# Softmax on Trainium2: the normalization fused with the split of the probabilities into two float16 parts

## The chip, the cores and the metric

The kernel runs on one core of a Trainium2 chip. The metric is the device time of one execution in microseconds (us); the time of a kernel is the median of its runs. The engines are named as the profile names them: PE (TensorE, matrix products; PEld is its weight load), DVE (VectorE), ACT (ScalarE), POOL (GpSimd) and SP (SyncE, which issues every DMA of this kernel). SBUF is the core's working memory, PSUM the memory into which PE writes.

## What is computed

Attention with a causal window of 128 keys and a linear bias, then two gated blocks. Cut to what matters:

```python
scores = (q @ k.T) / sqrt(64)                       # 4 batches, 8 heads, 576 tokens, 64 features
scores = where(mask, scores + bias, -1e9)            # mask: the query's own key and the 127 before it
attn = exp(scores - max(scores, axis=-1))
attn = attn / (sum(attn, axis=-1) + 1e-9)
x = attn @ v                                         # then heads side by side: [2304, 512]
x = (x @ w_a) * (x @ w_b) @ w_out                    # 512 -> 1536 -> 512
x = ((x @ w1) * (x @ w2) @ w3) @ w_out2              # 512 -> 1024 -> 1024 -> 512
```

The change concerns the division by the sum and what makes `attn` ready for the product with `v`.

## The kernel before

Attention is cut into 16 units (a batch and a pair of heads), and each unit into 5 steps of up to 128 query rows; there are 80 steps. The two heads of a pair are the index `j`. In steps 1 to 3 of a unit each head has 128 queries against 256 keys, so that its tile is 128x256; in step 0 there are 128 keys (128x128 for each head); in the last step 64 queries of both heads lie below each other in one 128x256 tile. So a unit has 7 head tiles of 128x256 and 2 of 128x128, and the kernel has 112 and 32 of them.

One step runs through these functions and lines:

- `scores` (L313): PE forms the scores in PSUM.
- `exps`: DVE adds the bias and takes the row's extremum (L325, with a short read of the accumulator after it), ACT takes the exponential and its sum (L331). The result is `pe`, float32, in SBUF; the statistics are in `st`.
- `norms`: two short DVE instructions turn the sum into the factor `st` (L344, L347). The factor holds a power of two that `pv_out` takes out again.
- `probs`: DVE multiplies `pe` by the factor in place (L357, one instruction for each head). The product is then split into two float16 parts that stand in `pp`: the first is a rounded copy (L363, on ACT; L361, on DVE, in step 0 alone), the second is what the copy lacks (`sub` on POOL, recorded at the helper's line L73, as are other subtractions: those of `v`, of the weights, of the gated product). A DMA then transposes `pp` into `pt` (L366).
- `pv` (L388): PE multiplies `pt` with three parts of `v`. `pv_out` (L400 on ACT, L401 on DVE) writes the token rows for the gated blocks, again as a rounded part and a rest.

The tiles `pe`, `st`, `pp` and `pt` have 4 buffers each, the scores 3 PSUM banks. Beside this, DVE and ACT split the transposed q and k (`qkh`, `qkl`, L278, L279), POOL splits `v` (128x640, two instructions for each unit), six weight tiles are converted (L107 to L132, tiles `ca` and `ce`), and PE does products of the first gated block where attention leaves it room (`Filler`, L521 to L551).

In which order the steps' functions are written down is set by `attention_ops`: the probabilities of a step come two steps after its scores, the product with `v` eight steps after them. From that, a scheduler of the programming layer sets the order of every engine's queue by a modelled timeline, so an edit to one instruction can move many others. Each engine works through its own queue in order. All transposes and loads stand in SP's queue.

After attention the kernel converts the other weights on ACT, DVE and POOL (L107 to L132), forms `w3 @ w_out` (L439) and runs the gated blocks (L521, L541, L559).

Of the kernel before, what the change touches and what calls it, by code (L numbers as in the profile page):

```python
# [15 lines left out]
ACTF = mybir.ActivationFunctionType  # L16
# [4 lines left out]
# Float32 products run as three float32r passes: an operand x is the exact sum of  # L21
# hi = float32r(x) and lo = x - hi, and x*w = lo*hi' + hi*lo' + hi*hi' to float32's accuracy.
# The second block's w3 @ w_out is formed first: (g @ w3) @ w_out = g @ (w3 @ w_out).
# Weights come as float64: their words are put together as rounded float32 on the chip.
# [6 lines left out]
GROUPS = (6, 4)  # groups of two 128-column chunks of each block's inner features  # L31
TA, TN = 256, 512  # tokens of a tile: beside attention, and after it
HALF = 1280  # the token at which the accumulators are cut in two
LAG, NLAG = 8, 2  # steps of attention from the scores to the product with v, and to the norms
AT = (0, 0, 1, 3)  # steps of a unit at which the next one is transposed
V_AT = {2: 1, 6: 2}  # steps at which the second and the third unit's v are loaded
FILL = 0.75  # microseconds of the first group's products in a step of attention
PACE = (0.3, 0.6)  # turns of the weights' conversion in a step: the first batch, the others
TURN = 400  # tokens of a chunk for each turn later
# [4 lines left out]
def attention_moe_moe(ctx, tc, q, k, v, w_a, w_b, w_o, w_1, w_2, w_3, w_o2, out):  # L44
# [27 lines left out]
    def sub(eng, out, a, b):  # L72
        eng.tensor_tensor(out=out, in0=a, in1=b, op=ALU.subtract)  # L73
# [5 lines left out]
    # ---------------------------------------------------------------- weights  # L79
    def load_cols(w, c):  # L80
        """128 columns of a [512, .] weight: [128, 4 * 128] with the rows on 4 x 128 partitions."""
# [7 lines left out]
    def load_rows(w, r, c):  # L89
        """128 rows and 512 columns."""  # L90
# [7 lines left out]
    def convert(raw, hi=None, lo=None, use=()):  # L98
        """Float64's two words as float32, to the nearest (0 below float32's exponents), and its
        split: stages, to be emitted one after the other, each when the one before has run."""  # L100
# [41 lines left out]
    class Stages:  # L142
        """Parts (load, stages of what it loads): a part's stages are emitted in turns one after
        the other, its load ahead of them; its second stage is the last to read the load."""
# [33 lines left out]
    # ---------------------------------------------------------------- attention  # L178
# [16 lines left out]
    def consts():  # L195
# [5 lines left out]
        # c - p - 128 for key column c of the window and query row p  # L201
# [13 lines left out]
        # the bias of each head, as the unscaled scores take it: a power of 2 times up to 8 bits  # L215
# [4 lines left out]
        # and for the two heads of a pair below each other  # L220
# [14 lines left out]
    def load_unit(u, which=(0, 1, 2)):  # L235
        b, hp = units[u]
        for x in which:
# [13 lines left out]
            # the last block of q has its two heads on the diagonal, zeros beside them  # L251
# [4 lines left out]
    # q's blocks and k's side by side, as many of them at a time as a bank takes  # L256
# [4 lines left out]
    def prep(u):  # L261
        """Functions that transpose and split a unit's q, k and v: (tensor engine, others)."""
# [20 lines left out]
        def v_parts():  # L283
            # v's three bfloat16 parts: the upper half of v, of what is left of it, and of what is left then
# [12 lines left out]
    def window(i):  # L297
        """Query rows, keys and key blocks of a query block; the groups of heads that it has side
        by side: the last block's rows are half as many, its two heads fill the partitions."""
        m = P if i < NB - 1 else LAST  # L300
        nb = 1 if i == 0 else 2
        return m, nb * P, nb, 2 if m == P else 1
# [451 lines left out]
```

## Time and profile before

| | |
|---|---|
| median of 3 runs | 1056.13 us (1048.25 to 1060.08) |
| the profiled execution, first to last instruction | 1056.7 us |
| attention, up to its last product with `v` | about 282 us |
| busy over the whole span | PE 1017.9, DVE 691.0, ACT 382.0, POOL 494.3 us |
| instructions on POOL | 409 |

The profiled execution is 0.6 us longer than the median, so its times can be set against the median as they stand. A busy time is the time in which an engine had at least one instruction under way; a PE that is busy is not PE at its peak, since its instructions overlap and may run at either of two clocks (2.4 GHz where the granted clock is 1.00, 1.2 GHz where it is 0.5; a stretch with both lies between). A wait of an engine costs only if the engine is the one that others wait for, so the chain of waits is read beside the busy times.

### The profile page before, as it was taken

The numbers are of one execution on the slowest core, as the hardware profiler recorded it, in microseconds if no ns is written. First come the engines' busy times: TensorE is split into PE (matmuls) and PEld (weight loads), VectorE is DVE, ScalarE is ACT, GpSimd is POOL, SyncE is SP. The second block draws the span as 40 slices with busy tenths as digits, with TensorE's granted clock in tenths as the row PEclk, the third lists the DMA queues.
The fourth block names the chain that finished last, engine by engine and source line by source line (L and its number), as shares of the span: only waits on it lengthen the run. The fifth ranks groups of instructions, "written<-read, shape, count | busy, mean of one in ns | idle before, by whom it ended". The sixth has DMA issues, their size and how long they took to land.

```text
span 1056.7 us, 16482 instructions
## 1 busy us (share of the span) xinstructions
PE 1017.9 (96%) x6162; PEld 838.2 (79%) x6162; DVE 691.0 (65%) x1420; ACT 382.0 (36%) x929; POOL 494.3 (47%) x409
## 2 busy tenths in 40 slices
PE   7889999999999889999999999999999999999998
PEld 5567788787987778887788788888888888888886
DVE  6999997757499995587969659565273373322222
ACT  5555766655344232332333323233322221211110
POOL 6566645445267562264636226477572352421111
PEclk9688979878899899999999999999999999999999
DMA  6867676656333221232232223121021020000012
GB/s 140 170 122 154 118 114 121 123 101 115 81 100 100 79 100 70 74 107 73 99 109 84 77 71 99 60 80 41 1 80 40 20 81 20 20 1 1 11 70 100
DMA packets 160080, 85.23 MB, mean 81 GB/s; under 512 B 128000, under 2 KB 148992, under 8 KB 160000
## 3 DMA queue, kind: packets, MB, share of 16 engines
q1 hardware_dynamic: 160000, 84.18, 31.5%
q8 instruction: 48, 0.79, 0.3%
q14 instruction: 32, 0.26, 0.1%
HBM read 58.20 MB, written 8.91 MB: 64 GB/s over the span
## 4 chain that ended last, share of the span: by engine, by line
PE 62%; DVE 22%; DMA 6%; issue 6%; ACT 2%; POOL 1%; SPq 1%; DVEq 0%; ACTq 0%; POOLq 0%
PE mm L521 33%; PE mm L559 10%; PE mm L541 7%; DVE ca L117 4%; PE tr L388 4%; PE mm L439 4%; PE s L313 3%; DVE pe L357 3%; DVE ca L120 3%; DVE ca L113 2%; DVE ce L123 2%; DMA pt<-pp 2%; DVE ce L127 2%; DMA raw<-in_moe_w_out 1%; DVE pe L325 1%
## 5 line engine op out<-in xcount | busy, mean ns | idle before, releaser
L73 POOL TENSOR_TENSOR gl<-g,gh 128x512 fp32r<-128x512 f32 (+1 forms) x108 | 127.7, 1183 | 265.3 <-ACT gh L531 258.4
L132 POOL TENSOR_TENSOR ca<-ca,ce 128x512 f32<-128x512 f32 x76 | 104.7, 1378 | 138.2 <-DVE ce L127 127.4
L528 DVE TENSOR_TENSOR g<-a,mm 128x512 f32<-128x512 f32 (+1 forms) x108 | 64.1, 594 | 157.3 <-PE mm L521 146.7
L531 ACT ACTIVATE gh<-g 128x512 fp32r<-128x512 f32 (+1 forms) x108 | 60.4, 559 | 209.4 <-DVE g L528 209.1
L73 POOL TENSOR_TENSOR pp<-pe,pp 128x512 f16<-128x512 f32 (+1 forms) x80 | 81.8, 1030 | 73.1 <-ACT pp L363 39.9
L521 PE MATMUL mm<-x_hi,wlA 128*128 128x512 f32 (+1 forms) x464 | 109.2, 356 | 0.0
L521 PE MATMUL mm<-x_lo,whA 128*128 128x512 f32 (+1 forms) x464 | 106.9, 351 | 0.0
L521 PE MATMUL mm<-x_hi,whA 128*128 128x512 f32 (+1 forms) x464 | 106.2, 349 | 0.0
L521 PE MATMUL mm<-x_hi,wlB 128*128 128x512 f32 (+1 forms) x400 | 99.8, 371 | 5.5 <-DVE g L528 5.0
L526 ACT ACTIVATE a<-mm 128x512 f32<-128x512 f32 (+1 forms) x108 | 56.1, 519 | 126.6 <-PE mm L521 126.5
L521 PE MATMUL mm<-x_lo,whB 128*128 128x512 f32 (+1 forms) x400 | 98.8, 369 | 0.0
L521 PE MATMUL mm<-x_hi,whB 128*128 128x512 f32 (+1 forms) x400 | 98.7, 369 | 0.0
L521 PEld LDWEIGHTS mm<-x_lo,whA 128*128 128x128 f32 x464 | 80.3, 197 | 10.5
L521 PEld LDWEIGHTS mm<-x_hi,whA 128*128 128x128 f32 x464 | 79.7, 196 | 11.1
L113 DVE TENSOR_SCALAR ca<-ca 128x512 f32<-128x512 f32 x76 | 48.8, 642 | 60.4 <-ACT ca L107 60.4
L521 PEld LDWEIGHTS mm<-x_hi,wlA 128*128 128x128 f32 x464 | 78.6, 195 | 12.1 <-issue 0.6
L107 ACT ACTIVATE ca<-raw 128x512 f32<-128x512 f32 x76 | 50.9, 669 | 101.5 <-DMA raw<-in_moe_w 51.6
L521 PEld LDWEIGHTS mm<-x_hi,wlB 128*128 128x128 f32 x400 | 70.6, 188 | 19.9 <-DVE g L528 6.1
L117 DVE SCALAR_TENSOR_TENSOR ca<-raw,ca 128x512 int32<-128x512 int32 x76 | 82.4, 1084 | 1.6
L357 DVE TENSOR_SCALAR pe<-pe,st 128x256 f32<-128x256 f32 (+1 forms) x144 | 81.5, 602 | 1.3
L331 ACT ACTIVATE pe<-pe,st 128x256 f32<-128x256 f32 (+1 forms) x144 | 68.7, 478 | 37.6 <-DVE st L325 36.0
L120 DVE SCALAR_TENSOR_TENSOR ca<-raw,ca 128x512 int32<-128x512 int32 x76 | 80.9, 1065 | 1.5
(100 smaller groups left out, 2086.7 us busy)
## 6 DMA issues: line engine op xcount, KB each, us to landing
raw<-in_moe_w SPq DMA_DIRECT2D x32, 512.0 KB, 3.5
raw<-in_moe_w_out SPq DMA_DIRECT2D x20, 512.0 KB, 3.5
raw<-in_moe_w_a SPq DMA_DIRECT2D x12, 512.0 KB, 3.5
raw<-in_moe_w_b SPq DMA_DIRECT2D x12, 512.0 KB, 3.5
out<-acc SPq DMA_DIRECT2D x18, 256.0 KB, 2.0
q_raw<-in_q SPq DMA_DIRECT2D x32, 128.0 KB, 2.6
k_raw<-in_k SPq DMA_DIRECT2D x32, 128.0 KB, 2.8
v_raw<-in_v SPq DMA_DIRECT2D x32, 128.0 KB, 2.6
```

The lines of the kernel that those rows point to most:

```text
L73: eng.tensor_tensor(out=out, in0=a, in1=b, op=ALU.subtract)
L113: nc.vector.tensor_scalar(out=a, in0=a, scalar1=bits(0x38100000), scalar2=bits(0x3FFFFFF8), op0=ALU.is_ge, op1=ALU.mult,)
L117: nc.vector.scalar_tensor_tensor(out=ai, in0=hw, scalar=3, in1=ai, op0=ALU.logical_shift_left, op1=ALU.bitwise_and)
L120: nc.vector.scalar_tensor_tensor(out=ai, in0=hw, scalar=-(1 << 30), in1=ai, op0=ALU.bitwise_and, op1=ALU.bitwise_or)
L132: nc.gpsimd.tensor_tensor(out=a, in0=a, in1=es[0], op=ALU.add)
L331: nc.scalar.activation(pe[:, j, :n], pe[:, j, :n], ACTF.Exp, bias=st[:, 0, j:j + 1], scale=-1.0, accum_out=st[:, 1, j:j + 1],)
L357: nc.vector.tensor_scalar(out=pe[:, j, :n], in0=pe[:, j, :n], scalar1=st[:, j:j + 1], scalar2=None, op0=ALU.mult)
L521: nc.tensor.matmul(p, w[:, z, kk, :], x[:, kk, o], start=(y == 0), stop=(y == len(terms) - 1))
L528: nc.vector.tensor_tensor(out=gg, in0=a, in1=ps[1], op=ALU.mult)
L531: nc.scalar.activation(gh, gg, ACTF.Copy)
L541: nc.tensor.matmul(p, w, x, start=(y == 0), stop=(y == len(terms) - 1))
L559: nc.tensor.matmul(p, x, w, start=(y == 0), stop=(y == len(terms) - 1))
```

## The change

The multiplication in place goes. The first float16 part becomes a copy with the factor as the copy's scale, one instruction for each head: on ACT in steps 1 to 4, on DVE in step 0 (`tensor_scalar` with a float16 output). The second part becomes one DVE instruction for each head, which multiplies `pe` by the factor and subtracts the first part (`scalar_tensor_tensor`). POOL has no part in the probabilities any more. The diff also drops comments, which is left out here.

```diff
 def probs(u, i):
     ...
         for j in range(nj):
-            nc.vector.tensor_scalar(
-                out=pe[:, j, :n], in0=pe[:, j, :n], scalar1=st[:, j:j + 1], scalar2=None, op0=ALU.mult
-            )
-        if i == 0:
-            nc.vector.tensor_copy(out=pp[:, :, 0, :], in_=pe[:, 0:nj, :n])
-        else:
-            nc.scalar.activation(pp[:, :, 0, :], pe[:, 0:nj, :n], ACTF.Copy)
-        sub(nc.gpsimd, pp[:, :, 1, :], pe[:, 0:nj, :n], pp[:, :, 0, :])
+            if i == 0:
+                nc.vector.tensor_scalar(
+                    out=pp[:, j, 0, :], in0=pe[:, j, :n], scalar1=st[:, j:j + 1], scalar2=None, op0=ALU.mult
+                )
+            else:
+                nc.scalar.activation(pp[:, j, 0, :], pe[:, j, :n], ACTF.Copy, scale=st[:, j:j + 1])
+        for j in range(nj):
+            nc.vector.scalar_tensor_tensor(
+                out=pp[:, j, 1, :], in0=pe[:, j, :n], scalar=st[:, j:j + 1], in1=pp[:, j, 0, :],
+                op0=ALU.mult, op1=ALU.subtract,
+            )
         t = sm_p.tile([P, 8 * P], F16, name="pt", bufs=4)[:, 0:2 * nj * n]
         nc.sync.dma_start_transpose(
```

In the changed kernel the new instructions have the lines L359 (`tensor_scalar`, 32 of them), L363 (ACT, 112 in place of 64) and L365 (`scalar_tensor_tensor`, 144); every line behind them is 4 higher than before. POOL has 80 instructions fewer (329), DVE 16 more (1436 in place of 1420), ACT 48 more. PE and SP have as many as before.

The scheduler sets other orders now. On DVE, in the middle of the third unit, before (numbers behind a name tell buffers apart; ISA is the bias and extremum of L325):

```order
L325 ISA pe_809,st_810<-s_770,relb2_94 128x256
L325 ISA st_810 128x1
L347 RECIPROCAL st_717<-st_717 128x2
L357 TENSOR_SCALAR pe_716<-pe_716,st_717 128x256 x2
L344 TENSOR_SCALAR st_765<-st_765 128x2
L347 RECIPROCAL st_765<-st_765 128x2
L113 TENSOR_SCALAR ca_416<-ca_416 128x512
L401 SCALAR_TENSOR_TENSOR x_lo_68<-tr_739,x_hi_67 128x128
L357 TENSOR_SCALAR pe_764<-pe_764,st_765 128x256 x2
```

The same place of the same unit now, on DVE:

```order
L347 RECIPROCAL st_664<-st_664 128x2
L347 RECIPROCAL st_715<-st_715 128x2
L405 SCALAR_TENSOR_TENSOR x_lo_68<-tr_737,x_hi_67 128x128
L123 TENSOR_SCALAR ce_407<-ca_314 128x512
L344 TENSOR_SCALAR st_763<-st_763 128x2
L344 TENSOR_SCALAR st_808<-st_808 128x1
L127 SCALAR_TENSOR_TENSOR ce_407<-raw_312,ce_407 128x512
L347 RECIPROCAL st_763<-st_763 128x2
L347 RECIPROCAL st_808<-st_808 128x1
L365 SCALAR_TENSOR_TENSOR pp_730<-pe_663,st_664,pp_730 128x256 x2
L365 SCALAR_TENSOR_TENSOR pp_774<-pe_714,st_715,pp_774 128x256 x2
```

The multiplication stood right behind its factor; the new instruction stands several instructions behind it, since ACT's copy comes between.

On ACT, for the same steps, before (`x_hi` is L400's output, `pe` the exponentials):

```order
L331 ACTIVATE pe_809,st_810<-pe_809,st_810 128x256
L400 ACTIVATE x_hi_67<-tr_783 128x128
L363 ACTIVATE pp_732<-pe_665 128x2x256
L363 ACTIVATE pp_776<-pe_716 128x2x256
L400 ACTIVATE x_hi_67<-tr_830 128x128
L363 ACTIVATE pp_823<-pe_764 128x2x256
```

And now, on ACT:

```order
L404 ACTIVATE x_hi_67<-tr_737 128x128
L331 ACTIVATE pe_762,st_763<-pe_762,st_763 128x256
L331 ACTIVATE pe_807,st_808<-pe_807,st_808 128x256
L363 ACTIVATE pp_730<-pe_663,st_664 128x256 x2
L363 ACTIVATE pp_774<-pe_714,st_715 128x256 x2
L404 ACTIVATE x_hi_67<-tr_781 128x128
L404 ACTIVATE x_hi_67<-tr_828 128x128
L363 ACTIVATE pp_821<-pe_762,st_763 128x256 x2
```

The copies stand at nearly the same places of ACT's queue, behind the same exponentials; each is now two instructions and needs the factor, not the product.

## Rows read from the trace of the kernel before

**Rows 1.** Busy time by stretch: length, then busy us (instructions) of each engine.
```profile
core 0: us, PE busy (x) PEld busy (x) DVE busy (x) ACT busy (x) POOL busy (x), PEclk, DMA share, GB/s
0.00:282.00 282.00, 262.21 (x2504) 207.43 (x2505) 226.38 (x787) 166.26 (x539) 154.04 (x154) 0.84 0.65 124
...
26.00:125.00 99.00, 88.31 (x831) 66.70 (x832) 94.23 (x292) 59.79 (x188) 60.77 (x53) 0.80 0.71 141
125.00:172.00 47.00, 47.00 (x456) 38.77 (x455) 41.60 (x148) 30.12 (x103) 23.52 (x23) 0.85 0.66 116
...
201.00:223.00 22.00, 21.97 (x149) 17.24 (x149) 11.98 (x52) 10.81 (x37) 9.15 (x10) 0.53 0.57 106
```

**Rows 2.** The chain that ended last, by line: 0 to 282 us, then 282 to 400.
```profile
by line: PE tr L388 14.1%; PE s L313 13.0%; DVE pe L357 11.3%; issue 9.6%; PE mm L521 9.3%; DMA pt<-pp 6.0%; DVE pe L325 4.6%; PE tr L274 3.9%; PE mm L541 2.8%; DMA q_raw<-in_q 2.8%; DVE st L344 2.7%; DVE x_lo L401 1.6%; DVE ca L117 1.5%; D
...
by line: DVE ca L117 20.1%; issue 17.6%; DVE ce L123 12.0%; DVE ca L120 11.5%; DVE ce L127 7.6%; DVE ca L113 6.5%; DVE acc L548 4.6%; POOL ca L132 4.0%; DMA raw<-in_moe_w_a 3.0%; DVE g L528 3.0%; DMA raw<-in_moe_w_out 3.0%; PE mm L521 2.7%;
```

**Rows 3.** Timeline, DVE then POOL, 94 to 98 us: start, duration, instruction.
```profile
94.08 2.03 DVE L357 TENSOR_SCALAR pe<-pe,st 128x256 f32<-128x256 f32 x2
...
97.24 1.14 DVE L344 TENSOR_SCALAR st<-st 128x2 f32<-128x2 f32 x1
...
94.65 1.31 POOL L73 TENSOR_TENSOR v<-v_raw 128x640 f32<-128x640 f32 x1
95.92 1.32 POOL L73 TENSOR_TENSOR wlA<-ca,whA 128x512 fp32r<-128x512 f32 x1
97.19 1.16 POOL L73 TENSOR_TENSOR pp<-pe,pp 128x512 f16<-128x512 f32 x1
```

**Rows 4.** Three lines of DVE, 0 to 282 us: duration ns min/median/max.
```profile
L357 DVE TENSOR_SCALAR pe<-pe,st x144: 271/352/1425, 11.1 to 269.0; 128x256 f32<-128x256 f32 x112, 128x128 f32<-128x128 f32 x32
...
L344 DVE TENSOR_SCALAR st<-st x80: 127/164/1264, 10.7 to 268.5; 128x2 f32<-128x2 f32 x64, 128x1 f32<-128x1 f32 x16
...
L117 DVE SCALAR_TENSOR_TENSOR ca<-raw,ca x6: 674/1036/1648, 28.6 to 102.8; 128x512 int32<-128x512 int32 x6
```

**Rows 5.** Groups by form, 0 to 282 us: count | busy us, mean ns | idle before.
```profile
L357 DVE TENSOR_SCALAR pe<-pe,st 128x256 f32<-128x256 f32 x112 | 67.1, 634 | 1.0
...
L363 ACT ACTIVATE pp<-pe 128x512 f16<-128x512 f32 x48 | 29.9, 625 | 19.4 <-DVE pe L357 14.3 <-DMA pt<-pp 4.8
...
L344 DVE TENSOR_SCALAR st<-st 128x2 f32<-128x2 f32 x64 | 22.6, 353 | 8.5 <-ACT pe L331 8.2
...
L401 DVE SCALAR_TENSOR_TENSOR x_lo<-tr,x_hi 128x128 fp32r<-128x128 f32 x64 | 17.9, 280 | 6.6 <-ACT x_hi L400 6.4
...
L357 DVE TENSOR_SCALAR pe<-pe,st 128x128 f32<-128x128 f32 x32 | 14.5, 490 | 0.3
...
L117 DVE SCALAR_TENSOR_TENSOR ca<-raw,ca 128x512 int32<-128x512 int32 x6 | 6.6, 1100 | 0.0
L363 ACT ACTIVATE pp<-pe 128x256 f16<-128x256 f32 x16 | 6.6, 410 | 3.7 <-DVE pe L357 2.8 <-DMA pt<-pp 0.9
L361 DVE CAST pp<-pe 128x256 f16<-128x256 f32 x16 | 5.5, 342 | 4.6 <-DMA pt<-pp 3.5 <-issue 1.1
L528 DVE TENSOR_TENSOR g<-a,mm 128x256 f32<-128x256 f32 x13 | 5.4, 416 | 8.6 <-PE mm L521 8.5
```

**Rows 6.** The page's costliest groups: POOL's part of the split.
```profile
L73 POOL TENSOR_TENSOR pp<-pe,pp 128x512 f16<-128x512 f32 (+1 forms) x80 | 81.8, 1030 | 73.1 <-ACT pp L363 39.9
```

**Rows 7.** Waits, 0 to 282 us: total us, times, longest us.
```profile
POOL pp L73 <- ACT pp L363: 39.9, 31, 3.4
...
DVE x_lo L401 <- ACT x_hi L400: 10.2, 15, 1.3
...
DVE st L344 <- ACT pe L331: 9.2, 16, 1.3
...
DVE qkl L279 <- ACT qkh L278: 7.3, 7, 3.6
...
ACT pp L363 <- DMA pt<-pp: 5.8, 8, 1.8
```

## The prediction

> **What bounds the kernel now.** I read the busy times by stretch first, then the chain of waits, then the groups of instructions by form, and the timeline where two of them met. The change touches attention alone, so the first question is how much of the time is attention and which engine sets its pace. It takes about 282 us; in the 146 us from 26 to 172 DVE is busy 94.2 of 99 us and 41.6 of 47, while ACT and POOL have room and PE, though busy, runs at a mean clock of 0.80 to 0.85 [rows 1]. Over all of attention DVE is busy 226.4 of 282 us. The chain agrees: 11.3% of attention's length ends on the multiplication by the factor (L357), more than on any other line that is not PE's, and 2.7% on the tiny L344, which handles two numbers in a row of the tile [rows 2]. Behind 282 us the chain lies on the conversion of weights on DVE; what is left to do there is the same before and after, since PE's queue has the same 3971 instructions ahead of the last product with `v`, so I let that part shift and not change.
>
> Why two simple lines cost so much is seen in the timeline [rows 3]. Two multiplications start at 94.08 while POOL works, and the pair takes 2.03 us; POOL's `v` instruction runs from 94.65 to 95.96. At 97.24 an L344 starts beside POOL's half of the split, which runs from 97.19 to 98.35, and ends with it: 1.14 us, where half of all L344 take 0.164 or less [rows 4]. So a DVE instruction that works from SBUF to SBUF, and meets one of POOL's, waits for it. Lines of DVE with an operand in PSUM show nothing of the kind: L401 has a mean of 280 ns, L528 of 416 [rows 5].
>
> **What the collisions cost, and what POOL's 80 instructions have of it.** I take the mean less what an undisturbed one takes. L357 on 128x256: the mean is 634 ns [rows 5], the median of all 144, of which 112 are of this size, 352 [rows 4]: 112 x 0.282 = 31.6 us. L357 on 128x128: 490 less the least value 271: 32 x 0.219 = 7.0. L344: 353 less the median 164, 64 x 0.189 = 12.1. L117: 1100 less 674, 6 x 0.426 = 2.6. Together 53.3 us of DVE's time. POOL is busy 154.0 us in attention [rows 1], of which the subtraction that goes is 81.8 [rows 6], or 53%. Given the same share of the collisions, it causes **28.3 us**. The bounds are 0 (what is left on POOL meets DVE as often as before) and all 53.3; I take the share, as POOL keeps its 32 `v` instructions and the weights'.
>
> **What DVE does instead.** 112 new instructions of 128x256 replace 112 multiplications of 352 ns. The trace of before has no such instruction of this size; the nearest are L528, 416 ns, with the same count of elements, and L401, 280 ns on 128x128, the same operation with one operand in PSUM [rows 5]. Both operands in SBUF cost no more: from 280 and 416 a line through 512 elements gives 688 ns, and L117 with two SBUF operands takes 674 at the least [rows 4]. So 112 x (416 - 352) = 7.2 us, 32 x (280 - 271) = 0.3, and in step 0, 32 multiplications on 128x128 of 271 ns, 8.7 us, in place of L361's 5.5 us [rows 5]. Sum **+10.7 us**. The low bound is 0 (as fast as the multiplication); the high one comes from L117, where collisions added 0.426 each against 0.282 for L357: 0.144 more on 144 instructions, times the 47% of POOL's work that stays, is 10 us on top.
>
> This sum can be weighed against a rule. The Trainium skill, "VectorE: DVE Perf Modes", section "The TRN2 errata", gives 58 cycles and the element count divided by the mode's factor at 0.96 GHz, and its tier table has float32 `tensor_scalar` at twice the rate of an instruction with two tensors. By that estimate the multiplication takes 194 ns and the new one 327, 133 ns apart, which would make 15 us of the 7.2 and put the forecast 6 us later; the rows show 64 ns between the forms, and I keep to them.
>
> **ACT and the new wait.** ACT now makes 112 copies of 128x256 at 410 ns, 45.9 us, in place of 48 x 0.625 + 16 x 0.410 = 36.6 [rows 5]: +9.4 us on an engine that is busy 166 of 282 us [rows 1], hidden beside DVE, and on the path only where DVE waits for a copy. That wait is new: DVE's second half of a split stands behind ACT's first half, in DVE's queue, and what is queued behind it (the next bias and extremum, on which ACT's exponentials and PE's score banks wait) is held too. In steps 1 to 4 of the 16 units there are 64 such places. DVE has three of the same kind today: x_lo behind x_hi waits 10.2 us in 80 instructions, L344 behind the exponential 9.2 in 80, qkl behind qkh 7.3 in 48 [rows 7]. That is 26.7 / 208 = 0.128 us each, so 64 x 0.128 = **+8.2 us**. The order speaks for a wait of this size and not more: the new instructions stand some ten places behind their factor, with DVE's other work between. The bounds are 0 and the 39.9 us that POOL now waits for the same copies.
>
> **The sum.** DVE: -28.3 + 10.7 + 8.2 = -9.4 us. From 26 to 172 us it counts in full; in the other 110 us of steady attention DVE is busy about two thirds of the time [rows 1] and I count somewhat under half. Weighted by length that is about 0.75, so -7 us. The profiled execution (1056.7) is 0.6 above the median, so I work from the median: 1056.1 - 7 = **1049 us**. POOL's 81.8 us come free off the path. The transposes are as many as before, and issue from the same queue.
>
> **Rivals.** *The relief runs through.* DVE never waits for the copies, and PE is fed without pauses: -28.3 + 10.7 = -17.6, of which some 16 reach the end. From 201 to 223 us PE is busy all the time and has a mean clock of 0.53 [rows 1], nearly all at 1.2 GHz, behind a stretch in which it waited for DVE; an attention with fewer stalls may have half of that, worth about 5 us. Together 1035, with 1040 where the clock gives nothing. For it: DVE is saturated for 146 us, and POOL has nothing that DVE waits for. Against it: PE's share of the chain is large [rows 2], and a new order can lose the clock elsewhere.
>
> *Something else paces attention.* PE's lines L388 and L313 have 27% of the chain and DMA pt<-pp 6.0% [rows 2]; ACT's copy itself waits 5.8 us for a transpose to free its `pp` [rows 7]. If DVE's gain only turns into waits for these, the time is 1053 to 1059.
>
> *Slower: DVE takes POOL's place as the engine that waits for ACT.* POOL waited 39.9 us for the copies, 31 times and up to 3.4 us [rows 7], at no cost, since nobody stood behind it. In DVE's queue all of softmax stands behind. The mechanism decides from a mean wait of 17.6 / 64 = 0.28 us a step, about twice what the three present waits have. With all 39.9 us it is (39.9 - 17.6) x 0.75 = +17, 1073 us; with 0.4 us a step it is 1062. Against it speaks the distance in the order; for it, that ACT's copies stand behind two `x_hi` that wait for PE.
>
> That the change doesn't do what it says is excluded: POOL's queue has 80 instructions fewer.
>
> **Chances.** The forecast (1043 to 1054) 0.41; the relief runs through (1033 to 1043) 0.30; something else paces (1053 to 1059) 0.14; slower 0.15. The three runs shown lie within 12 us, so about 1%, 10.6 us, is what a measurement can tell from no change. Faster by more than that is below 1045.6: the second case and a fifth of the first, 0.38. Slower by more is above 1066.7: most of the last case, 0.12. In between 0.50. The range reaches from 1035 to 1064: it leaves out the best part of the second case and about half of the last.
>
> **What the profile after would show.** L344's mean falls from 353 ns to some 250; the new L365 on 128x256 has a floor near 0.41 us and a mean under 0.6; POOL is busy about 72 us in attention; DVE's busy time there is near 209 us; waits of L365 for L363 sum to 5 to 15 us; attention ends near 275 us and what follows keeps its length. I am wrong if L365's floor lies above 0.5 us, if its waits for L363 exceed 20 us, if L344 and L117 collide as often with what POOL keeps, or if DVE's time falls as forecast and attention ends at 282 us all the same, which the chain would put on PE or the transposes.

## The result and the profile after

The changed kernel takes 1043.58 us (median of 18 runs, 1035.01 to 1048.17), the kernel before 1053.61 us on the same chips (median of 18). The ratio is 0.9916, with an interval of 0.989 to 0.9941: faster by 0.6 to 1.1%, 10.0 us by the medians. One run of the kernel before, far off the others at 1209.77 us, does not enter the ratio. The two profiled executions differ by more, 1056.7 and 1040.8 us of span, since the first lies above its median and the second below it; so of the 15.9 us between the traces about 6 are chance. (A span is some 1.8 us shorter than the time of the same execution: 1040.8 and 1042.55 us in the changed kernel.)

Busy time by stretch in the changed kernel, attention first (columns as in [rows 1]):

```profile
0.00:262.00 262.00, 247.43 (x2501) 194.70 (x2502) 215.19 (x803) 176.57 (x587) 76.47 (x74) 0.86 0.71 133
26.00:125.00 99.00, 92.65 (x839) 69.28 (x839) 90.44 (x317) 66.94 (x220) 32.14 (x25) 0.76 0.76 151
125.00:172.00 47.00, 45.68 (x521) 37.52 (x519) 38.70 (x151) 33.24 (x114) 10.66 (x10) 0.96 0.66 128
201.00:223.00 22.00, 21.61 (x256) 17.94 (x257) 18.67 (x79) 17.54 (x62) 5.09 (x5) 1.00 0.79 139
...
262.00:1040.00 778.00, 757.42 (x3663) 631.75 (x3661) 464.49 (x634) 215.51 (x390) 339.14 (x255) 1.00 0.20 65
```

And in the kernel before, what comes behind attention, same columns:

```profile
282.00:1056.00 774.00, 755.71 (x3660) 630.74 (x3658) 464.64 (x633) 215.74 (x390) 340.31 (x255) 1.00 0.20 65
```

The last product with `v` ends at 261.6 us where it ended at 281.3. POOL's busy time in attention has fallen from 154.0 us [rows 1] to 76.5, DVE's from 226.4 to 215.2, and ACT's has risen from 166.3 to 176.6. What follows holds the same work (PE 757.4 and 755.7 us, DVE 464.5 and 464.6) and takes 779.2 us in place of 775.4, so 3.8 of the 19.7 us are given back. The second profile of the changed kernel (E0 below) has 779.3 there, and the other kernels of the table below lie between 773.7 and 778.8; where these 3.8 us come from was not traced.

Most of the gain in attention shows as shorter busy time of PE: the same 2499 products up to the last one with `v` keep it busy for 247.1 us where it was 261.4, at a mean granted clock of 0.86 in place of 0.84. How much of this is the clock and how much are shorter waits between products, no run here parts.

The chain of waits of the changed kernel, 0 to 262 us, by line:

```profile
by line: PE mm L525 15.7%; PE tr L392 15.7%; PE s L313 11.9%; DMA pt<-pp 6.6%; issue 5.5%; PE mm L545 5.3%; PE tr L274 4.9%; DVE pp L365 2.0%; DVE pp L359 1.4%; DVE pe L325 1.0%; ACT pp L363 0.8%; DVE st L344 0.6%; ACT pe L331 0.5%; DVE qkl
```

The multiplication had 11.3% of this chain and L344 2.7% [rows 2]; their places now are L365 with 2.0 and L344 with 0.6. What attention ends on has moved further to PE: the products with `v` (L392), the scores (L313), and the first gated block's products that fill PE's gaps (L525, L545).

The groups by form, DVE, ACT and POOL, 0 to 282 us of the changed kernel (columns as in [rows 5]):

```profile
L365 DVE SCALAR_TENSOR_TENSOR pp<-pe,st,pp 128x256 f16<-128x256 f32 x112 | 64.9, 603 | 7.0 <-ACT pp L363 6.5
...
L344 DVE TENSOR_SCALAR st<-st 128x2 f32<-128x2 f32 x64 | 17.6, 274 | 1.8 <-ACT pe L331 1.6
...
L365 DVE SCALAR_TENSOR_TENSOR pp<-pe,st,pp 128x128 f16<-128x128 f32 x32 | 13.5, 452 | 0.0
L359 DVE TENSOR_SCALAR pp<-pe,st 128x128 f16<-128x128 f32 x32 | 12.4, 417 | 9.8 <-DMA pt<-pp 9.8
...
L363 ACT ACTIVATE pp<-pe,st 128x256 f16<-128x256 f32 x112 | 51.2, 500 | 14.5 <-DMA pt<-pp 5.6 <-issue 1.7 <-DVE st L325 1.4
...
L73 POOL TENSOR_TENSOR v<-v 128x640 bf16<-128x640 f32 x16 | 20.9, 1305 | 1.2
L73 POOL TENSOR_TENSOR v<-v_raw 128x640 f32<-128x640 f32 x16 | 20.7, 1291 | 55.2 <-PE tr L392 35.4 <-DMA k_raw<-in_k 11.0 <-DMA v_raw<-in_v 8.7
```

Their least, median and greatest durations in ns, as in [rows 4]:

```profile
L365 DVE SCALAR_TENSOR_TENSOR pp<-pe,st,pp x144: 323/478/1544, 12.2 to 251.1; 128x256 f16<-128x256 f32 x112, 128x128 f16<-128x128 f32 x32
...
L344 DVE TENSOR_SCALAR st<-st x80: 129/158/1212, 10.0 to 249.0; 128x2 f32<-128x2 f32 x64, 128x1 f32<-128x1 f32 x16
...
L359 DVE TENSOR_SCALAR pp<-pe,st x32: 271/282/1301, 10.9 to 242.2; 128x128 f16<-128x128 f32 x32
```

Collisions are still there, with what POOL keeps. The timeline of the changed kernel, DVE then POOL, around 45 and 53 us:

```profile
45.08 0.41 DVE L325 CUSTOM_DVE_ANT_0 pe<-s,relb 128x256 f32<-128x256 f32 x1
...
52.18 0.47 DVE L365 SCALAR_TENSOR_TENSOR pp<-pe,st,pp 128x256 f16<-128x256 f32 x1
...
52.91 1.28 DVE L365 SCALAR_TENSOR_TENSOR pp<-pe,st,pp 128x256 f16<-128x256 f32 x1
...
44.48 1.26 POOL L73 TENSOR_TENSOR v<-v 128x640 bf16<-128x640 f32 x1
...
52.64 1.27 POOL L73 TENSOR_TENSOR wlA<-ca,whA 128x512 fp32r<-128x512 f32 x1 [2.28 <-ACT whA L139]
```

The L365 at 52.18 meets nobody and takes 0.47 us. The one at 52.91 meets POOL's subtraction (until 53.91) and takes 1.28. The L325 at 45.08, which reads the scores from PSUM, runs inside POOL's instruction (44.48 to 45.74) at its usual 0.41. The Trainium skill, "SBUF — State Buffer", section "Who interferes with whom", says the same: DVE and GpSimd share one pair of ports, whichever comes later is blocked for the whole of the other's instruction, and a DVE instruction with one SBUF input outside the two-port modes is free of it. These rows agree with both halves of it.

The waits of the changed kernel, 0 to 282 us (columns as in [rows 7]):

```profile
DVE pp L359 <- DMA pt<-pp: 9.8, 9, 2.5
DVE x_lo L405 <- ACT x_hi L404: 9.5, 11, 1.6
...
DVE qkl L279 <- ACT qkh L278: 7.1, 6, 3.6
...
DVE pp L365 <- ACT pp L363: 6.5, 13, 0.9
ACT gh L535 <- DVE g L532: 6.2, 6, 2.0
ACT pp L363 <- DMA pt<-pp: 5.6, 8, 1.0
```

The new wait of DVE for ACT's copy is 6.5 us in 13 places, none above 0.9. POOL's wait of 39.9 us has not passed to DVE. In the second profile of the same program (E0), the same wait is longer, in the waits from 0 to 282 us:

```profile
DVE pp L365 <- ACT pp L363: 11.7, 16, 1.9
```

### The profile page after: what moved, and what is told of

The parts are those of the page before. It is cut to its first block, busy times and chain, and to the rows that moved or that the text cites. A ratio compares the mean times of both kernels' runs of the same rounds, so it can differ in the third digit from the quotient of the medians.

```text
span 1040.8 us, 16528 instructions
## 1 busy us (share of the span) xinstructions
PE 1004.9 (97%) x6162; PEld 826.5 (79%) x6162; DVE 679.7 (65%) x1436; ACT 392.1 (38%) x977; POOL 415.6 (40%) x329
## 3 DMA queue, kind: packets, MB, share of 16 engines
q1 hardware_dynamic: 160000, 84.18, 32.4%
## 4 chain that ended last, share of the span: by engine, by line
PE 71%; DVE 11%; issue 4%; DMA 4%; ACT 1%; POOL 0%; DVEq 0%; ACTq 0%; POOLq 0%; SPq 0%
PE mm L525 39%; PE mm L545 10%; PE mm L563 10%; PE mm L443 4%; PE tr L392 4%; PE s L313 3%; DVE ca L117 3%; DVE ca L120 2%; DMA pt<-pp 2%; DVE ca L113 1%; DVE ce L123 1%; PE tr L274 1%; DMA raw<-in_moe_w_out 1%; DVE ce L127 1%; DVE acc L552 1%
## 5 line engine op out<-in xcount | busy, mean ns | idle before, releaser
L532 DVE TENSOR_TENSOR g<-a,mm 128x512 f32<-128x512 f32 (+1 forms) x108 | 64.0, 593 | 154.0 <-PE mm L525 142.1
L535 ACT ACTIVATE gh<-g 128x512 fp32r<-128x512 f32 (+1 forms) x108 | 60.3, 559 | 211.1 <-DVE g L532 211.0
L525 PE MATMUL mm<-x_hi,wlA 128*128 128x512 f32 (+1 forms) x464 | 109.3, 355 | 0.4 <-ACT acc L550 0.4
L525 PE MATMUL mm<-x_hi,wlB 128*128 128x512 f32 (+1 forms) x400 | 100.2, 372 | 7.3 <-DVE g L532 6.1
L525 PE MATMUL mm<-x_lo,whA 128*128 128x512 f32 (+1 forms) x464 | 105.9, 347 | 0.0
L525 PE MATMUL mm<-x_hi,whA 128*128 128x512 f32 (+1 forms) x464 | 104.2, 346 | 0.0
L525 PE MATMUL mm<-x_lo,whB 128*128 128x512 f32 (+1 forms) x400 | 98.9, 369 | 0.0
L525 PE MATMUL mm<-x_hi,whB 128*128 128x512 f32 (+1 forms) x400 | 98.3, 368 | 0.0
L525 PEld LDWEIGHTS mm<-x_hi,wlA 128*128 128x128 f32 x464 | 78.1, 193 | 13.1 <-ACT acc L550 0.6
L525 PEld LDWEIGHTS mm<-x_hi,wlB 128*128 128x128 f32 x400 | 70.9, 189 | 21.6 <-DVE g L532 7.1
L525 PEld LDWEIGHTS mm<-x_lo,whA 128*128 128x128 f32 x464 | 78.7, 193 | 10.9 <-issue 0.2
L525 PEld LDWEIGHTS mm<-x_hi,whA 128*128 128x128 f32 x464 | 78.3, 193 | 10.9 <-issue 0.4
L365 DVE SCALAR_TENSOR_TENSOR pp<-pe,st,pp 128x256 f16<-128x256 f32 (+1 forms) x144 | 78.3, 570 | 7.0 <-ACT pp L363 6.5
L525 PEld LDWEIGHTS mm<-x_lo,whB 128*128 128x128 f32 x400 | 71.4, 189 | 13.0
L525 PEld LDWEIGHTS mm<-x_hi,whB 128*128 128x128 f32 x400 | 71.1, 189 | 12.6
L331 ACT ACTIVATE pe<-pe,st 128x256 f32<-128x256 f32 (+1 forms) x144 | 68.5, 477 | 28.3 <-DVE st L325 27.9
L120 DVE SCALAR_TENSOR_TENSOR ca<-raw,ca 128x512 int32<-128x512 int32 x76 | 78.0, 1026 | 1.5
```

The lines of the kernel that those rows point to most:

```text
L120: nc.vector.scalar_tensor_tensor(out=ai, in0=hw, scalar=-(1 << 30), in1=ai, op0=ALU.bitwise_and, op1=ALU.bitwise_or)
L331: nc.scalar.activation(pe[:, j, :n], pe[:, j, :n], ACTF.Exp, bias=st[:, 0, j:j + 1], scale=-1.0, accum_out=st[:, 1, j:j + 1],)
L365: nc.vector.scalar_tensor_tensor(out=pp[:, j, 1, :], in0=pe[:, j, :n], scalar=st[:, j:j + 1], in1=pp[:, j, 0, :], op0=ALU.mult, op1=ALU.su ...
L525: nc.tensor.matmul(p, w[:, z, kk, :], x[:, kk, o], start=(y == 0), stop=(y == len(terms) - 1))
L532: nc.vector.tensor_tensor(out=gg, in0=a, in1=ps[1], op=ALU.mult)
L535: nc.scalar.activation(gh, gg, ACTF.Copy)
```

## The experiments

Twelve kernels ran beside the kernel before; E7 has no attention and is not in the table, and there is no E3 and no E6. Each edit gives the scheduler another order for all queues, so two kernels differ by their edit and by an order. The table is in the order of the text: the time, the ratio to the kernel before with its interval, the end of attention in the profiled execution, DVE's busy time up to there, and the mean of L344 on 128x2, which does next to nothing itself and so shows the collisions.

| kernel | median us | ratio | attention | DVE busy | L344, ns |
|---|---|---|---|---|---|
| before | 1053.61 | 1 | 281.3 | 226.2 | 353 |
| changed | 1043.58 | 0.9916 (0.989 to 0.9941) | 261.6 | 215.1 | 274 |
| E0 changed again | 1042.53 | 0.9884 (0.9847 to 0.992) | 256.6 | 208.7 | 262 |
| E1 dead POOL half | 1068.04 | 1.0114 (1.0077 to 1.0151) | 290.6 | 253.3 | 376 |
| E2 half moved to DVE | 1045.35 | 0.9909 (0.9882 to 0.9937) | 268.5 | 229.2 | 290 |
| E4 no half at all | 1039.03 | 0.9826 (0.9782 to 0.987) | 247.8 | 193.9 | 283 |
| E5 constant factor | 1044.24 | 0.993 (0.9903 to 0.9957) | 264.9 | 205.6 | 331 |
| E8 L344 on ACT | 1042.88 | 0.9898 (0.9865 to 0.9931) | 269.3 | 199.2 | on ACT |
| E9 dead, one column | 1040.23 | 0.9877 (0.9831 to 0.9923) | 270.3 | 208.7 | 284 |
| E10 one column in the path | 1043.62 | 0.9887 (0.9853 to 0.9922) | 262.2 | 211.0 | 312 |
| E11 dead POOL work, no waits | 1060.57 | 1.0072 (1.0041 to 1.0103) | 280.1 | 234.6 | 389 |
| E12 the same work on DVE | 1067.46 | 1.0149 (1.0118 to 1.018) | 286.6 | 249.6 | 287 |
| E13 half of E12's | 1054.15 | 1.003 (0.9998 to 1.0062) | 276.0 | 231.2 | 293 |

Below, "the changed kernel" is the mean of its two ratios, 0.990, with DVE busy for 211.9 us, and a step of 0.001 in the ratio is 1.05 us. Attention's end is from one execution each and moves by several us between executions (E0 and the changed kernel are one program), so the comparisons go by ratios. E4's traced execution is the fastest of its six, by 9.6 us.

**E0. The changed kernel once more,** beside E1, E2 and E4.

> The changed kernel itself, so that the others of this group can be compared with it on the same chip. Both theories: 0.989 to 0.994 of the kernel before, as its first 18 runs had.

It took 0.9884 of the kernel before (0.9847 to 0.992), in line with the first comparison.

**E1. Give POOL its work back.** The changed kernel, with the old subtractions beside the new instructions, into a tile that nobody reads:

```diff
+        junk = sm_p.tile([P, 2 * 2 * P], F16, name="junk", bufs=1)[:, 0:nj * n].rearrange("p (a c) -> p a c", a=nj)
+        sub(nc.gpsimd, junk, pe[:, 0:nj, :n], pp[:, :, 0, :])
```

> The changed kernel, with POOL's 80 subtractions put back as dead work: they read pe and the first part and write a tile that nobody reads. Theory 1 (the change gains because DVE no longer collides with POOL's subtractions): L344's mean goes back from 275 ns to about 350, L365's from 570 to above 700, DVE loses 20 to 28 us in attention and the time rises by 15 to 20 us over the changed kernel, so it is slower than the kernel before. Theory 2 (the gain lies in the shorter path from the factor to the transpose, or in the new order of the queues): the dead work is off every path, and the time stays within 4 us of the changed kernel's.

Ratio 1.0114, some 22 us above the changed kernel: more than the whole gain is gone, and a little more than the 15 to 20 us expected, as DVE's busy time rose by 41 us and not by 20 to 28. The groups of E1, 0 to 285 us:

```profile
L365 DVE SCALAR_TENSOR_TENSOR pp<-pe,st,pp 128x256 f16<-128x256 f32 x112 | 92.3, 848 | 3.9 <-ACT pp L363 3.7
...
L344 DVE TENSOR_SCALAR st<-st 128x2 f32<-128x2 f32 x64 | 24.1, 376 | 1.4 <-ACT pe L331 1.4
```

The same L365 takes 848 ns in place of 603, and L344 376 in place of 274. But the dead work also keeps `pe` and `pp` from being free, and waits in POOL's queue, so three causes were still open; E9, E10 and E11 part them.

**E2. Move the half and fuse nothing.** The kernel before with one word changed:

```diff
-        sub(nc.gpsimd, pp[:, :, 1, :], pe[:, 0:nj, :n], pp[:, :, 0, :])
+        sub(nc.vector, pp[:, :, 1, :], pe[:, 0:nj, :n], pp[:, :, 0, :])
```

> The kernel before with the subtraction moved from POOL to DVE, and nothing fused: the multiplication in place and the copy of its product stay. Theory 1: DVE wins 28 us of collisions and gets 48 instructions of 128x512 at about 0.69 us and 32 of 256 elements a row at 0.42, 46 us, so +18 us of DVE time, +13 us in all: 1064 to 1070, or 1.01 of the kernel before. The fusion is then needed for the gain. Theory 3 (to free POOL is enough, DVE has room): at or below the kernel before, 0.99 to 1.00.

Ratio 0.9909, as fast as the changed kernel. The theory that DVE's time sets the pace had 1064 to 1070 us here and missed by 19; the one by which it is enough to free POOL hit. The groups of E2, 0 to 285 us:

```profile
L357 DVE TENSOR_SCALAR pe<-pe,st 128x256 f32<-128x256 f32 x112 | 46.1, 450 | 0.1
...
L73 DVE TENSOR_TENSOR pp<-pe,pp 128x512 f16<-128x512 f32 x48 | 34.7, 725 | 0.8 <-ACT pp L363 0.8
L344 DVE TENSOR_SCALAR st<-st 128x2 f32<-128x2 f32 x64 | 18.5, 290 | 1.2 <-ACT pe L331 1.1
...
L73 DVE TENSOR_TENSOR pp<-pe,pp 128x256 f16<-128x256 f32 x32 | 14.9, 464 | 1.9 <-ACT pp L363 1.9
```

DVE has taken on 49.6 us of subtractions and sees L357's mean fall from 634 ns [rows 5] to 450, and ends up as busy as before (229.2 and 226.2 us), yet the kernel is 9.6 us faster. So the fusion with the normalization is not what gains; taking the half off POOL is.

**E4. No second half anywhere.** The kernel before without POOL's subtraction; the rests are zeros, so this part of the computation is left out. `pp` has five buffers of its own, one for each step of a unit, cleared once:

```diff
+    for x in pps:
+        nc.vector.memset(x, 0.0)
 ...
-        sub(nc.gpsimd, pp[:, :, 1, :], pe[:, 0:nj, :n], pp[:, :, 0, :])
```

> The kernel before without POOL's subtraction and with nothing in its place: the second parts of the probabilities are zeros that are written once at the start, so the rest of the split is left out; the transposes and the products with v stay as many. pp has five buffers by step in place of four in turn. Theory 1: the 23 to 28 us of collisions go and no DVE work comes: -17 to -21 us, 0.980 to 0.984 of the kernel before, faster than the changed kernel by 7 to 11 us, the price of the longer DVE instructions and of their waits. Theory 2: L344 and L357 still wait as long (for POOL's other work), and the time is within 4 us of the changed kernel's or of the kernel before's.

Ratio 0.9826, where 0.980 to 0.984 was expected. With the half gone altogether some 18 us are to be had (14 to 23 by the interval); the changed kernel has 10 of them.

**E5. The factor as a constant.** In the changed kernel, L365 takes a constant for the row's factor, so that the rest is a wrong number:

```diff
-                out=pp[:, j, 1, :], in0=pe[:, j, :n], scalar=st[:, j:j + 1], in1=pp[:, j, 0, :],
+                out=pp[:, j, 1, :], in0=pe[:, j, :n], scalar=0.125, in1=pp[:, j, 0, :],
```

> The changed kernel with the constant 0.125 in place of the row's factor in the second part alone (the rest of the split is then a wrong number; nothing else differs). Theory a (the factor read from SBUF costs 56 ns): L365's floor on 128x256 falls from 472 to 416 ns, 112 x 56 + 32 x 55 = 8 us of DVE time, -4 to -6 us of time. Theory b (the float16 operand): floor and time as in the changed kernel, within 3 us.

The median of L365 falls from 478 to 419 ns, as expected of the theory that the factor's reading costs, but the time does not: 0.993. Some 6 us of DVE's busy time went and no gain in time can be seen. L344's mean is 331 ns here, so some collisions moved to it.

**E7. The forms by themselves.** A kernel without attention (its output is zeros): each form 8 times by itself, then 8 times with a POOL subtraction of 128x512 queued beside each. `mult` is L53, `rest` L56, `rest` with a constant L61, `rest` on 128x128 L66, float32 operands L72 and L77, no factor at all L82, two numbers in a row L85. POOL's instructions are L95.

> No attention at all: eight forms of DVE instruction, 8 times each with POOL idle, then 8 times each beside POOL subtractions of 128x512 from SBUF; the output is zeros, everything else of the computation is left out. L365 took at least 472 ns in the changed kernel where 416 was forecast. Theory a (the factor read from SBUF for each row costs the 56 ns): the second part with the factor takes about 470, with a constant 416, in float16 and float32 alike. Theory b (the float16 operand or output costs it): the float32 forms take 416 with either factor, the float16 ones 470. Theory c (it is a remainder of collisions): all take 416 with POOL idle. Beside POOL, theory 1 has every form, the two-column one too, wait for the end of a POOL instruction: means 0.4 us and more above the quiet ones.

Both halves together, least, median and greatest duration in ns:

```profile
L53 DVE TENSOR_SCALAR f<-pe,st x16: 231/342/347, 3.8 to 32.1; 128x256 f32<-128x256 f32 x16
...
L56 DVE SCALAR_TENSOR_TENSOR o<-pe,st,hi x16: 467/476/480, 5.7 to 35.2; 128x256 f16<-128x256 f32 x16
...
L61 DVE SCALAR_TENSOR_TENSOR o<-pe,hi x16: 406/412/419, 8.9 to 37.9; 128x256 f16<-128x256 f32 x16
...
L66 DVE SCALAR_TENSOR_TENSOR o<-pe,st,hi x16: 342/843/1349, 11.6 to 47.1; 128x128 f16<-128x128 f32 x16
...
L72 DVE SCALAR_TENSOR_TENSOR f<-pe,st,hf x16: 475/976/1482, 13.7 to 58.2; 128x256 f32<-128x256 f32 x16
...
L77 DVE SCALAR_TENSOR_TENSOR f<-pe,hf x16: 414/945/1482, 16.9 to 69.4; 128x256 f32<-128x256 f32 x16
...
L85 DVE TENSOR_SCALAR os<-st x16: 157/1203/1232, 22.2 to 90.6; 128x2 f32<-128x2 f32 x16
```

With the factor from SBUF 476 ns, with a constant 412; with float32 operands at the least 475 and 414. So the type is nothing and the factor is about 60 ns. How a collision looks is in E7's timeline of DVE:

```profile
26.82 1.22 DVE L85 TENSOR_SCALAR os<-st 128x2 f32<-128x2 f32 x1
27.96 0.34 DVE L53 TENSOR_SCALAR f<-pe,st 128x256 f32<-128x256 f32 x1
28.22 1.22 DVE L85 TENSOR_SCALAR os<-st 128x2 f32<-128x2 f32 x1
```

An instruction on two numbers a row, 157 ns when alone, takes 1.22 us, as it waits out POOL's.

L53, L56 and L61 were not held up, though POOL had an instruction under way all the time: there POOL waited. Its durations, as above, then one of its instructions and the eight L61 beside it, from the timelines:

```profile
L95 POOL TENSOR_TENSOR gc<-ga,gb x64: 1256/1307/7287, 22.5 to 111.3; 128x512 f32<-128x512 f32 x64
...
32.17 7.29 POOL L95 TENSOR_TENSOR gc<-ga,gb 128x512 f32<-128x512 f32 x1
...
35.58 2.75 DVE L61 SCALAR_TENSOR_TENSOR o<-pe,hi 128x256 f16<-128x256 f32 x8
```

While DVE's L56 and L61 followed each other without a gap, from 32.4 to 38.3 us, one POOL instruction took 7.29 us in place of 1.31. So the wait goes both ways, and a collision costs whichever engine comes second.

**E8. L344 on ACT.** In the changed kernel the small instruction that collides most goes to ACT (which leaves out the 1e-9 that it adds):

```diff
-        nc.vector.tensor_scalar(
-            out=st[:, 2], in0=st[:, 1], scalar1=1.0e-9, scalar2=1.0 / PSC, op0=ALU.add, op1=ALU.mult
-        )
+        nc.scalar.activation(st[:, 2], st[:, 1], ACTF.Copy, scale=1.0 / PSC)
```

> The changed kernel with L344 moved to ACT (a scaled copy of two columns; the 1e-9 is below the rounding of a sum that is at least 1, and is left out). In the changed kernel L344 still takes 17.6 us on 64 two-column instructions, 7 of them beyond its floor, beside POOL's v. Theory 1 (DVE's time sets the pace of attention): DVE loses 20 us of instructions, ACT gains 80 short ones of about 0.2 us, and the reciprocal now waits for ACT: -6 to -12 us against the changed kernel. Theory 4 (PE, the transposes or the latency of a step set the pace now): within 3 us of the changed kernel, or slower, as one more change of engine lies on each step's path.

DVE's busy time falls by 12.7 us, the time by nothing that shows (0.9898). The theory that less work on DVE gains on missed a second time.

**E9. The waits of POOL's queue without its work,** and **E10. a third engine in the path without its work.** E9 has 80 dead subtractions of one column for each head, which wait for ACT's copies as the old ones did; E10 a one-column copy on POOL behind the rest, for which the transposes must wait.

```diff
+        junk = sm_p.tile([P, 2], F16, name="junk", bufs=1)[:, 0:nj].rearrange("p (a c) -> p a c", a=nj)
+        sub(nc.gpsimd, junk, pe[:, 0:nj, 0:1], pp[:, :, 0, 0:1])
```

```diff
+        nc.gpsimd.tensor_copy(out=pp[:, :, 1, 0:1], in_=pp[:, :, 1, 0:1])
```

> The changed kernel with 80 dead subtractions on POOL of one column a head: they wait for ACT's copies as POOL's halves of the split did, and hold POOL's queue (v, the gated rest, the weights) as those did, but are over in about a tenth of the time. Theory 1 (the 1.2 us collisions cost the time): within 4 us of the changed kernel, 0.986 to 0.994 of the kernel before. Theory 5 (v and the gated rest stood in POOL's queue behind instructions that waited 40 us for ACT): half or more of the first dead work's 25 us comes back, 1.000 to 1.010.

> The changed kernel with 80 one-column copies on POOL of the second part onto itself, between DVE's new instruction and the transpose: each step's path runs through POOL's queue again, behind POOL's other work, at next to no time on POOL. Theory 1: within 4 us of the changed kernel, 0.986 to 0.994 of the kernel before. Theory 6 (the gain lies in the path of each step, which no longer passes POOL's queue): 8 to 12 us come back, 0.998 to 1.004.

0.9877 and 0.9887: neither costs anything that shows, though POOL waits for ACT's copies for 88.1 us in E9 (39.9 before) and for L365 for 78.9 us in E10. What stands behind a waiting POOL is not what the old half cost, nor is the longer path from the copy to the transpose.

**E11. The work without its waits.** In the changed kernel 80 dead subtractions of the old sizes on POOL, which read only the loaded `v_raw`:

```diff
+        junk = sm_p.tile([P, 4, P], F16, name="junk", bufs=1)[:, 0:nj * nb]
+        vr = v_raws[u % 3][:, 0:nj * nb, :]
+        sub(nc.gpsimd, junk, vr, vr)
```

> The changed kernel with 80 dead subtractions on POOL of the old sizes that read only v as it was loaded: they wait for nothing recent, nobody waits for them, and no step's path passes POOL. Only the collisions come back. Theory 1: as with the first dead work, 15 to 25 us over the changed kernel, 1.003 to 1.013 of the kernel before, and L365's mean back above 800 ns. Theories 5 and 6: within 4 us of the changed kernel, 0.986 to 0.994.

1.0072, some 18 us above the changed kernel. Nothing of the softmax waits for these instructions; they stand in DVE's way and in POOL's queue. That it is the queue, with `v` coming late for PE, the waits of E11 speak against: from 0 to 280 us this line and one of 0.2 us are all that PE waited for POOL.

```profile
PEld L395 <- POOL junk L73: 0.8, 1, 0.8
```

The groups of E11, 0 to 285 us:

```profile
L365 DVE SCALAR_TENSOR_TENSOR pp<-pe,st,pp 128x256 f16<-128x256 f32 x112 | 66.4, 618 | 8.3 <-ACT pp L363 7.8
...
L344 DVE TENSOR_SCALAR st<-st 128x2 f32<-128x2 f32 x64 | 24.9, 389 | 2.8 <-ACT pe L331 2.7
L359 DVE TENSOR_SCALAR pp<-pe,st 128x128 f16<-128x128 f32 x32 | 19.3, 636 | 3.6 <-DMA pt<-pp 3.6
...
L73 POOL TENSOR_TENSOR junk<-v_raw 128x512 f16<-128x512 f32 x48 | 50.9, 1060 | 1.8
```

L344 goes from 274 to 389 ns and L359 from 417 to 636. L365 itself, at 618, collides little more than in the changed kernel, where above 800 was expected: the dead work fell on other instructions. With E1 this makes the collisions the cause of the loss, at 18 to 22 us for 80 instructions.

**E12 and E13. Planned work on DVE in place of collisions.** E2, E5 and E8 spoke against DVE's time as the pace, E11 for it. E12 gives E11's dead subtractions to DVE, where the scheduler accounts for them; E13 only every second one.

```diff
-        sub(nc.gpsimd, junk, vr, vr)
+        sub(nc.vector, junk, vr, vr)
```

> The changed kernel with eighty dead subtractions of the old sizes, reading only v_raw, given to VectorE in place of GpSimd (E11 had the same ones on GpSimd); nothing reads what they write. They add about 39 us to VectorE's busy time inside the attention stage (48 of some 0.6 us, 32 of some 0.33). Theory 1a, that after the relief VectorE's time as such still paces the stage: the attention stage grows by 12 to 20 us as in E11, ratio to the kernel before 1.003 to 1.010. Theory 1b, that what costs are the unplanned waits at GpSimd's instructions, and that planned work on VectorE goes into its gaps: within 5 us of the changed kernel, ratio 0.986 to 0.995.

> The changed kernel with forty dead subtractions on VectorE, every second one of E12's, reading only v_raw. They add about 20 to 27 us of instruction time to VectorE in attention, as much as E11's collisions added to its busy time (20 to 26 us, for which the whole kernel took 17 to 20 us more). E12's eighty cost 26 us for some 41 us of busy time. Theory 1c, that each microsecond of VectorE's time costs the same, planned or not, at 0.6 of itself: 12 to 16 us above the changed kernel, ratio to the kernel before 1.000 to 1.005. Theory 1d, that some 15 to 20 us of planned VectorE time fit into its gaps in the changed kernel (as in E2), and only what is above that costs, while E11's unplanned waits cost from the first on: within 6 us of the changed kernel, ratio 0.986 to 0.994.

1.0149 and 1.003: the work costs, all of it and half of it. E12's dead groups, 0 to 285 us:

```profile
L73 DVE TENSOR_TENSOR junk<-v_raw 128x512 f16<-128x512 f32 x48 | 37.3, 777 | 0.0
...
L73 DVE TENSOR_TENSOR junk<-v_raw 128x256 f16<-128x256 f32 x32 | 15.9, 496 | 2.2 <-DMA v_raw<-in_v 2.2
```

They take 53 us by themselves, not the 39 expected. But DVE's busy time as a whole rose by 37.7 us, near what was expected, since L365 and others collide less than in the changed kernel (L365's mean on 128x256 is 559 ns). So E12 lies above its range by the price of a microsecond. Against the changed kernel's 211.9 us, E13 has 19.3 us more of DVE's busy time and costs 13.7 us (0.71 of it), E12 37.7 for 26.2 (0.70), E11 22.7 for 18.1 (0.80), E1 41.4 for 22.5 (0.54). Planned or not, a microsecond more on DVE costs 0.5 to 0.8 in these four. The theory that gaps swallow planned time falls as a general one; E2 (17.3 us more, 0.9 us later) stays as the exception, below.

## Why the prediction was right, and where its steps were not

- **What bounds attention.** Right: DVE's collisions with POOL's half. E11 brings the loss back with the work alone, E9 and E10 show that neither the queue nor the path did it. The work behind attention stayed, with 3.8 us given back that the forecast had not.
- **The relief, 28.3 of 53.3 us.** By the same working the rows after leave 112 x (603 - 478) = 14.0, 32 x (452 - 323) = 4.1 for L365, 64 x (274 - 158) = 7.4 for L344, 32 x (417 - 271) = 4.7 for L359, 30.2 us in all (without L117, 2.6 before). So some 20 to 23 went. Forecasting by POOL's share of busy time was near, a little too good.
- **The longer DVE instructions, +10.7 us: the term that was mis-sized.** L365's median is 478 ns (416 forecast), E7 has 342 at the least on 128x128 (280), and step 0's copy has a median of 282 (271): 112 x (478 - 352) + 32 x (342 - 271) + (32 x 282 - 5500) ns = 14.1 + 2.3 + 3.5 = 19.9 us. The nearest rows, L528 and L401, had everything but a factor read from SBUF for each row, and that is what costs 60 ns (E7, E5). The page that the prediction weighed, the Trainium skill's "VectorE: DVE Perf Modes", section "The TRN2 errata", had the difference of the two forms (133 ns by the estimate from its formula, 476 - 342 = 134 measured in E7), though the two durations by that formula, 194 and 327, are each some 150 ns short. The section says itself that the formula comes out too short for a single instruction. About half of the difference (64 ns) is the factor's, by E7, of which the rule says nothing. The rule's warning about the sum was good; that it would put the time 6 us later was not.
- **The new wait, +8.2 us.** 6.5 us in 13 places, 11.7 in 16 in E0. Right, by its mechanism and its size; the rival "slower" by 39.9 us of waits is refuted. ACT's copies were mis-sized too: 500 ns each (L363 above) where 410 was forecast; the copy of before, with its 410 ns on 128x256 [rows 5], had no factor to read for each row. That is 10 us more on ACT than forecast; what it costs the kernel, no run here parts.
- **The conversion, -9.4 x 0.75.** The term that carries least. With the two terms corrected, DVE's instructions and waits sum to about -22 + 20 + 6.5 = +4 us, and by the prediction's rule the kernel would have been no faster, some 3 us slower. DVE's busy time, which counts the overlap of neighbouring instructions once, fell by 11 us (17.5 in E0), the old wait of L344 for the exponential from 9.2 us [rows 7] to 1.8, and the time by 10. So the sum of durations was no good measure of what DVE gives free, and the closeness of 7 to 10 us is in part luck. For time that is added, 0.75 was near the mark (0.54 to 0.80 in E1, E11, E12, E13).
- **The marks.** L344's mean 274 (about 250 forecast), POOL 76.5 us (72), DVE 215.2 (near 209; E0 208.7), L365's waits 6.5 us (5 to 15), its mean 603 ns (below 600, just missed). L365's floor was forecast near 0.41 us and is 0.47 (E7), still below the 0.5 from which the prediction would have been wrong. Attention ended 20 us earlier in the profiles, where 7 was forecast; the medians say 10 for the whole kernel.
- **The rivals.** "The relief runs through" is the nearest: the measured median, 1043.6, lies at its slow end (1043), where the forecast's own band begins, and its sign that PE is fed better may show in 201 to 223 us (granted clock 1.00 in place of 0.53 [rows 1], though that stretch holds other work by now, 256 products in place of 149), while 26 to 125 us lost some (0.76 in place of 0.80). "Something else paces" holds for the next step: in the changed kernel, less work on DVE gains nothing (E5, E8), and the chain lies on PE.

**What stays open.** E2 and E13 have the same busy time on DVE (229.2 and 231.2 us) and like collisions (L344 at 290 and 293 ns) and lie 12.7 us apart. E2's ACT makes 48 copies of 128x512 in place of 96 of 128x256 and is busy 164.6 us up to attention's end, against 178.4 in E13; that ACT's time is paid for too is a guess that no run here parts from the effect of the order, since every edit reorders the queues. How much the order alone is worth was not measured: E0, E5, E8, E9 and E10, from 0.9877 to 0.993, are 5.6 us apart, no more than their intervals allow, and that is the scale of what these comparisons can't explain. Why less work on DVE gains nothing in E5 and E8, while more of it costs, is argued from the chain that now lies on PE and not shown by a run.

## What to carry to other kernels

Price a helper engine's work by what it does to its neighbour, not by its own idle time: POOL had room for the half, and its 80 instructions still cost the kernel 10 us, because DVE's work in SBUF waits where it meets them. When two tempting edits come together (moving the work and fusing it), run the plain move by itself: here it had the whole gain, within what the intervals can tell. And when the bound moves to another engine, the price for more time on the old one does not tell what less of it gives back: +19 us on DVE cost 14, -13 us gave nothing.

## What the runs showed of the hardware

- A `scalar_tensor_tensor` of 128x256 on DVE takes 476 ns with a factor read from SBUF for each row, 412 with a constant; with float32 in place of float16 for the second operand and the output it is 475 and 414 at the least (E7); the multiplication alone, with such a factor, takes 342.
- ACT's copy of 128x256 from float32 to float16 takes 410 ns without a factor [rows 5] and 500 with one read for each row (L363 of the changed kernel); no run has a constant there.
- Even a tiny instruction collides: one of two numbers a row goes from 157 ns to 1.22 us (E7). And POOL waits too: beside 16 instructions of DVE without a gap, one of its own takes 7.29 us in place of 1.31 (E7).
- Two executions of the changed program differ by 4.9 us of span, 1040.8 and 1035.9, and by 5.0 of them in attention (261.6 and 256.6). Their mean granted clock over the first 262 us is 0.86 (row above) and 0.91, in the windows of E0:

```profile
0.00:262.00 262.00, 247.09 (x2543) 195.82 (x2544) 209.89 (x805) 179.15 (x593) 77.00 (x74) 0.91 0.74 137
```

So the granted clock differs between two executions of one program, and the end of attention in a single profile is no finer measure than that.
